# A fused attention and two-layer feed-forward kernel: second layer's first two blocks by halves, stores by batch, weights staged in other places

## The chip, the cores and the metric

One core of a Trainium2 chip. The time is that of one execution on the device, in microseconds: 1831.82 in the median of 3 runs (1831.54 to 1834.25).

## The reference

```python
# q, k, v: (8 batches, 8 heads, 576, 64), float32; chunks of 64 positions attend within themselves
scores = scale * q_c @ k_c^T;  attn = softmax(scores);  x = attn @ v_c      # x: (4608, 512)
# layer 1 (rational): w_in (512, 2048), w_out (2048, 512), both float64
h = x @ w_in
g = (a0 + a1*h + a2*h^2 + a3*h^3) / (1 + |b0|*|h| + |b1|*h^2 + 1e-6)
x = g @ w_out
# layer 2 (squared relu), same sizes, own weights
g = s * max(x @ w_in2, 0)^2 + b
out = g @ w_out2                                                            # (4608, 512) float32
```

## The kernel before

The 4608 tokens are 9 blocks of 512 (one chunk of 64 positions of all 8 batches). A step is one slice of 128 of the 2048 hidden features for one block: `mm1` makes h (12 matrix products of 128x128 by 128x512, since each float32 operand is a high and a low part and three of the four products are kept), the elementwise functions `ew_a` to `ew_e` make g and split it into gh and gl, and `mm2` adds g times w_out to four PSUM banks (12 products more). `mm2` runs `LAG` = 2 steps behind `mm1`. There are 16 slices for each block, 9 blocks and 2 layers: 288 steps, 0 to 143 for layer 1 and 144 to 287 for layer 2. All is written out by hand in program order: the loop at line 617 issues the work of each step, and each engine and each DMA queue takes its own in that order.

In layer 1, blocks 0 and 1 take turns by halves (line 380): slices 0 to 7 of block 0, then of block 1, then 8 to 15 of each. A half's sum is copied from PSUM (`evac`), stored in scratch memory `x2d`, read back (`part_load`) and added to the second half's. All other blocks, those of layer 2 too, run their 16 slices in a row. Attention of later blocks is laid between the steps of layer 1 (`att_pe`, `att_out`); its q and k come by 16 loads of 32 KB (`att_load`, line 174, SP queue) that wait for the transposes of the tile before (lines 234, 235).

Weights are float64 and are turned into float32 on the chip. Each of 32 tiles a layer goes through these: `w_stage` loads 512 KB into one of four places of tag "big", which the copies out of PSUM use too; `w_ends` (ACT, two operations) and `w_words` (DVE lines 344, 346, 347, then POOL line 348) make the float32 word in one of three places of tag "w"; `w_split` makes high and low part (ACT line 353, then DVE or POOL line 354) in the place of a layer-1 weight that is no longer read. `due` sorts the tiles by the step that needs them, `WORDS` says how many begin in each step of the first 32. A tile that begins in step i has its words made at the end of step i and is split at the end of step i + 1, behind the words of the tiles that begin there. Loads are issued on ACT's queue in the loop, ahead of ACT's `ew_a`. In steps 132 to 157 the tiles of layer 2 are converted; its blocks' inputs come back from `x2d` (`x2_load`, `x2_split`).

At a block's end `evac` is issued in the step after the block's last `mm2`. Layer 2's sums go to the output with one store of 256 KB for a bank, whose rows are 2 batches of 64 (line 444). After the loop the last block's four banks are copied and stored.

Of the kernel before, what the change touches and what calls it, by code (L numbers as in the profile page):

```python
# [51 lines left out]


WORDS = (1, 1, 1, 1, 1, 1, 1, 1, 1, 1, 1, 1, 1, 1, 1, 1, 1, 1, 1, 1, 2, 2, 1, 0, 1, 0, 3, 0, 1, 0, 0, 0)
SPLIT = "VVVVGGVVVVVVVVVVVVVVGVVGVVGVGGGG"


@with_exitstack
def tile_chunk_attention__then__rational_ffn__then__relu2_ffn(
# [70 lines left out]
    def f(t):  # L130
        return t.bitcast(F32)
# [31 lines left out]
    def att_load(n):  # L163


        h0, s0 = heads(n)
        st = att.setdefault(n, {})
        for key, src in (("q", qkv[0]), ("k", qkv[1])):
            t = st[key] = ap_.tile([P, TB], F32, tag=key, name="qk")
            t = t.rearrange("t (p g d) -> t p g d", g=2, d=32)  # L170
# [58 lines left out]
    def att_turn(n):  # L229

        st = att[n]
        qT = st["qT"] = ap_.tile([P, 2, NP, CH], F32, tag="qT", name="qT")
        kT = st["kT"] = ap_.tile([P, 2, NP, CH], F32, tag="kT", name="kT")
        V.transpose(qT.rearrange("d c p t -> d (c p t)"), st["q"])
        V.transpose(kT.rearrange("d c p t -> d (c p t)"), st["k"])
# [137 lines left out]
    def x2_split(j, kk):  # L373
        xh, xl = xt[NB + j]
        A.activation(xh[:, kk], f(xl[:, kk]), AF.Copy)
        V.tensor_tensor(out=xl[:, kk], in0=f(xl[:, kk]), in1=f(xh[:, kk]), op=ALU.subtract)
# [35 lines left out]
    part = {}  # L412

    def part_load(jj):

        part[jj] = []
        for z in range(2):
            o = ap_.tile([P, 2, TB], F32, tag="big", name="o", bufs=4)
            SP.dma_start(out=o[:, 0, :], in_=x2d[jj][2 * z])
            SP.dma_start(out=o[:, 1, :], in_=x2d[jj][2 * z + 1])  # L420
            part[jj].append(o)

    def evac(jj):
        for z in range(2):
            acc = acc_t[jj][z]
            if jj in part:
                o = part[jj][z]
                V.tensor_tensor(out=o, in0=acc, in1=o, op=ALU.add)
            else:
                o = ap_.tile([P, 2, TB], F32, tag="big", name="o", bufs=4)  # L430
                if z == 0:
                    A.activation(o, acc, AF.Copy)
                elif jj < NB:
                    V.tensor_copy(o, acc)
                else:
                    V.tensor_copy(o[:, 0], acc[:, 0])
                    A.activation(o[:, 1], acc[:, 1], AF.Copy)
            for y in range(2):
                t = 2 * z + y
                if jj < NB:  # L440
                    SP.dma_start(out=x2d[jj][t], in_=o[:, y, :])
                else:
                    s0 = (jj - NB) * CH
                    SP.dma_start(
                        out=out.rearrange("(b s) d -> b s d", b=B)[2 * t:2 * t + 2, s0:s0 + CH, :],
                        in_=o[:, y, :],
                    )
        del acc_t[jj]
# [60 lines left out]
    with tc.manual_schedule():  # L509
# [19 lines left out]
        def w_stages(phase, n, dma):  # L529
            for _ in range(n):  # L530
                if wq:
                    kind, i = wq.pop(0)
                    staged.append((phase, kind, i, w_stage(phase, kind, i, dma)))

        def w_begin(n):
            now = [staged.pop(0) for _ in range(min(n, len(staged)))]
            return [(phase, kind, i, st, w_ends(st)) for phase, kind, i, st in now]

        def w_mid(now):
            for phase, kind, i, st, w in now:  # L540
                w_words(st, w)
# [72 lines left out]
        now = words  # L614
        att_load(NV)

        for i in range(NSTEP + LAG):
# [12 lines left out]
            e = i - (N1 - MF)  # L630
            if e == KD - 1:
# [11 lines left out]
            if i >= LAG:  # L643
# [9 lines left out]
            j, kk = divmod(e, MF)
            if 0 <= j < NB and kk == 1:
                x2_load(j)
            if 0 <= j < NB and 6 <= kk < 6 + KD:
                x2_split(j, kk - 6)
# [30 lines left out]
```

## Time and profile before

| | |
|---|---|
| median of 3 runs | 1831.82 us |
| profiled execution | 1833.56 us, span 1831.8 us |
| PE busy | 1715.9 us (94%) |
| DVE | 1129.8 us (62%) |
| ACT | 857.7 us (47%) |
| POOL | 648.2 us (35%) |
| granted TensorE clock, mean | 0.972 |

The span runs from the first to the last instruction. Busy PE is not PE at its peak, as matrix products overlap. By slices of the span PE is full from about 300 to 900 us and from 1100 to 1800 us, and DVE is fullest between 950 and 1100 us. An idle engine costs nothing where another sets the time.

### The profile page before, as it was taken

How to read it: one execution, taken by the hardware profiler on the slowest of the kernel's cores; microseconds unless marked ns; L12 is line 12 of the kernel's file. 1: busy time of each engine (PE TensorE's matmuls, PEld its weight loads, DVE VectorE, ACT ScalarE, POOL GpSimd, SP SyncE). 2: the span in 40 equal slices, each digit the busy share in tenths (PEclk: the TensorE clock that was granted, in tenths of full speed). 3: DMA queues.
4: the chain of work that ended last, by engine and by line, in shares of the span. 5: the costliest groups of instructions: out<-in, count | busy, mean ns of one | idle time of the engine just before them, and what ended most of it. 6: DMA issues, size and time to landing. Idle time of an engine off the chain costs nothing.

```text
span 1831.8 us, 25181 instructions
## 1 busy us (share of the span) xinstructions
PE 1715.9 (94%) x9482; PEld 1392.6 (76%) x9482; DVE 1129.8 (62%) x1789; ACT 857.7 (47%) x1389; POOL 648.2 (35%) x561
## 2 busy tenths in 40 slices
PE   6698689999999999999998889999999999999994
PEld 4577467888888888888876668888888888888883
DVE  5899778777787778777699993333333333333331
ACT  4677456556565656565677552222223222222221
POOL 2577556555655555555677440000000000000000
PEclk8899899999999999999999999999999999999997
DMA  8522332222121222221123321010000000000000
GB/s 199 125 81 92 89 85 63 54 35 57 29 56 31 57 35 59 35 56 21 58 80 115 127 81 47 5 42 23 24 23 24 24 24 27 20 32 15 14 10 23
DMA packets 204034, 96.03 MB, mean 52 GB/s; under 512 B 179848, under 2 KB 179848, under 8 KB 203912
## 3 DMA queue, kind: packets, MB, share of 16 engines
q1 hardware_dynamic: 196136, 66.11, 14.9%
q10 hardware_dynamic: 7776, 28.32, 4.8%
q8 instruction: 74, 1.21, 0.3%
q14 instruction: 48, 0.39, 0.1%
HBM read 73.40 MB, written 20.97 MB: 52 GB/s over the span
## 4 chain that ended last, share of the span: by engine, by line
PE 75%; DVE 13%; POOL 2%; ACT 2%; issue 2%; SPq 1%; DMA 1%; ACTq 0%; DVEq 0%; POOLq 0%
PE acc L410 36%; PE h L392 12%; PE h L394 12%; PE h L393 12%; DVE w L346 2%; PE pat L303 2%; DVE w L344 2%; DVE t L473 1%; DVE w L354 1%; DVE t L489 1%; DVE t L472 1%; DVE h L488 1%; DVE w L347 1%; DVE ah L487 1%; PE pat L246 1%
## 5 line engine op out<-in xcount | busy, mean ns | idle before, releaser
L392 PE MATMUL h<-xh,w 128*128 128x512 f32 x1152 | 460.4, 400 | 0.0
L394 PE MATMUL h<-xh,w 128*128 128x512 f32 x1152 | 451.1, 392 | 2.4 <-POOL w L354 2.4
L393 PE MATMUL h<-xl,w 128*128 128x512 f32 x1152 | 451.1, 392 | 0.0
L464 ACT ACTIVATE r<-h 128x512 f32<-128x512 f32 x144 | 85.9, 596 | 509.5 <-PE h L394 503.2
L410 PE MATMUL acc<-gh,w 128*128 128x512 f32 x1152 | 293.6, 397 | 30.7 <-POOL w L354 9.8
L410 PE MATMUL acc<-w,gh 128*128 128x512 f32 x1152 | 288.8, 393 | 12.2 <-DVE gh L504 5.9
L410 PEld LDWEIGHTS acc<-gh,w 128*128 128x128 f32 x1152 | 216.0, 190 | 83.4 <-ACT gh L501 13.0
L492 DVE TENSOR_SCALAR r<-r,s_sb,b_sb 128x512 f32<-128x512 f32 x144 | 86.6, 602 | 287.6 <-ACT r L465 287.6
L410 PEld LDWEIGHTS acc<-w,gh 128*128 128x128 f32 x1152 | 217.6, 189 | 59.7 <-issue 5.8
L394 PEld LDWEIGHTS h<-xh,w 128*128 128x128 f32 x1152 | 217.6, 189 | 49.5 <-POOL w L354 2.8
L392 PEld LDWEIGHTS h<-xh,w 128*128 128x128 f32 x1152 | 218.5, 190 | 47.1
L393 PEld LDWEIGHTS h<-xl,w 128*128 128x128 f32 x1152 | 218.2, 189 | 43.5
L459 POOL TENSOR_SCALAR r<-ah,ab_sb 128x512 f32<-128x512 f32 x144 | 112.0, 777 | 298.1 <-ACT ah L457 297.9
L460 POOL TENSOR_TENSOR r<-r,ah 128x512 f32<-128x512 f32 x144 | 186.7, 1297 | 12.0
L502 POOL TENSOR_TENSOR gl<-t,gh 128x512 fp32r<-128x512 f32 x144 | 188.1, 1306 | 6.1 <-ACT gh L501 6.1
L410 PE MATMUL acc<-gl,w 128*128 128x512 f32 x576 | 158.4, 398 | 6.1 <-POOL gl L502 6.1
L479 ACT ACTIVATE ah<-r,lnb 128x512 f32<-128x512 f32 x144 | 104.0, 722 | 117.0 <-POOL r L460 116.0
L410 PE MATMUL acc<-w,gl 128*128 128x512 f32 x576 | 156.3, 394 | 0.0
L487 DVE SCALAR_TENSOR_TENSOR ah<-r,h 128x512 f32<-128x512 f32 x144 | 98.4, 683 | 86.0 <-ACT h L480 86.0
L457 ACT ACTIVATE ah<-h 128x512 f32<-128x512 f32 x144 | 85.7, 595 | 134.8 <-PE h L394 124.3
L348 POOL TENSOR_TENSOR w<-w,wst 128x512 int32<-128x512 int32 x64 | 97.7, 1527 | 111.8 <-DVE w L347 73.4
L410 PEld LDWEIGHTS acc<-gl,w 128*128 128x128 f32 x576 | 110.1, 192 | 32.0 <-POOL gl L502 8.6
(81 smaller groups left out, 2051.8 us busy)
## 6 DMA issues: line engine op xcount, KB each, us to landing
wst<-in_moe_w_out_dram ACTq DMA_DIRECT2D x30, 512.0 KB
wst<-in_moe_w_in_dram ACTq DMA_DIRECT2D x24, 512.0 KB
x2d<-o SPq DMA_DIRECT2D x44, 256.0 KB
xl<-x2d SPq DMA_DIRECT2D x36, 256.0 KB
out_dram<-o SPq DMA_DIRECT2D x36, 256.0 KB
qk<-in_q_dram SPq DMA_DIRECT2D x224, 32.0 KB
qk<-in_k_dram SPq DMA_DIRECT2D x224, 32.0 KB
vs<-in_v_dram SPq DMA_DIRECT2D x56, 128.0 KB
```

Of the source, the lines that this page charges most:

```text
L348: G.tensor_tensor(out=w, in0=w, in1=low, op=ALU.add)
L392: T.matmul(h, wh, xh[:, kk], start=kk == 0, stop=False)
L393: T.matmul(h, wh, xl[:, kk], start=False, stop=False)
L394: T.matmul(h, wl, xh[:, kk], start=False, stop=kk == KD - 1)
L410: T.matmul(o, l, r, start=first and n == 0, stop=last and n == 2)
L459: G.tensor_scalar(out=r, in0=ah, scalar1=ab_sb[:, 1:2], scalar2=ab_sb[:, 0:1], op0=ALU.mult, op1=ALU.add)
L460: G.tensor_tensor(out=r, in0=r, in1=ah, op=ALU.mult)
L464: A.activation(r, h, AF.Relu)
L479: A.activation(ah, r, AF.Ln, scale=RS, bias=lnb)
L487: V.scalar_tensor_tensor(out=t, in0=r, scalar=ONE, in1=y, op0=ALU.add, op1=ALU.mult)
L492: V.tensor_scalar(out=r, in0=r, scalar1=s_sb, scalar2=b2_sb, op0=ALU.mult, op1=ALU.add)
L502: G.tensor_tensor(out=gl, in0=g, in1=f(gh), op=ALU.subtract)
```

## The change

- Layer 2's blocks 0 and 1 take turns by halves as layer 1's do; their half sums go through `x2d` again. `WORDS2` gives the number of tiles that begin in each step from 128 on, and `X2` the steps at which the inputs of layer 2 are loaded. For its second block the inputs' low part is made on POOL.
- `evac` only copies PSUM to SBUF, at the end of the step that holds the block's last `mm2`; `store`, in the next step, adds the first half's sum where there is one (two banks on POOL, two on DVE) and issues the stores. From layer 1's last block on, the copies lie in attention's places "v", "e" and "eT".
- Output stores: two of 128 KB for a bank, one for each batch.
- `mm2_last`: the last two steps' second products run bank by bank; each bank is copied (half on ACT, half on DVE) and stored (one batch on SP's queue, one on ACT's) while the next runs.
- Weight loads are issued on SP's queue at the end of the step, layer 2's also into the places "qk" and "qkT" of attention (each now one tile for q and k). "w" has four places. `w_end` (the split) is issued before `w_mid` (the words), and its engine in layer 2 is POOL up to step 144 and DVE after that, instead of by turns.
- Layer 2's scale and bias move from DVE to ACT.

```diff
+WORDS2 = (0, 0, 0, 1, 0, 0, 0, 0, 1, 0, 1, 0, 1, 0, 1, 1, 2, 1, 2, 1, 1, 2, 1, 2, 1, 1, 1, 1, 2, 1, 1, 1, 2, 1, 1, 1)
+X2 = (1, 16, 41) + tuple(range(52, 140, 16))
...
-        st = ap_.tile([P, TB, 2], I32, tag="big", name="wst", bufs=4)
+        tag = ("big" if phase == 0 else ("big", "qk", "big", "qkT", "big", "big")[next(turn) % 6])
+        st = ap_.tile([P, TB, 2], I32, tag=tag, name="wst", bufs=4 if tag == "big" else 1)
...
-        w = ap_.tile([P, TB], I32, tag="w", name="w", bufs=3)
+        w = ap_.tile([P, TB], I32, tag="w", name="w", bufs=4)
...
-    steps = [(j, y * HF + m, m == 0, m == HF - 1) for y in range(2) for j in range(2) for m in range(HF)]
-    steps += [(j, m, m == 0, m == MF - 1) for j in range(2, 2 * NB) for m in range(MF)]
+    steps = []
+    for j0 in (0, NB):
+        steps += [(j0 + j, y * HF + m, m == 0, m == HF - 1) for y in range(2) for j in range(2) for m in range(HF)]
+        steps += [(j0 + j, m, m == 0, m == MF - 1) for j in range(2, NB) for m in range(MF)]
...
+    def out_store(jj, t, o, dma=SP):
+        s0 = (jj - NB) * CH
+        for c in range(2):
+            row = (2 * t + c) * (NT // B) + s0
+            (SP, dma)[c].dma_start(out=out[row:row + CH, :], in_=o[c * CH:(c + 1) * CH, :])
+    def mm2_last():
+        jj = steps[-1][0]
+        for z in (0, 2, 1, 3):
+            acc = acc_t[jj][z // 2][:, z % 2, :]
+            for i in (NSTEP - 2, NSTEP - 1):
+                gh, gl = g_t[i]
+                wh, wl = w_out[1, steps[i][1]]
+                t = slice(z * P, (z + 1) * P)
+                for n, (w, g) in enumerate(((wh, gh), (wl, gh), (wh, gl))):
+                    T.matmul(acc, g[:, t], w, start=False, stop=i == NSTEP - 1 and n == 2)
+            o = ap_.tile([P, 2, TB], F32, tag="big", name="o", bufs=4)[:, 0]
+            hf = slice(0, TB // 2), slice(TB // 2, TB)
+            A.activation(o[:, hf[0]], acc[:, hf[0]], AF.Copy)
+            V.tensor_copy(o[:, hf[1]], acc[:, hf[1]])
+            out_store(jj, z, o, A)
...
+    def store():
+        for jj, t, o in sums:
             if jj in part:
-                o = part[jj][z]
-                V.tensor_tensor(out=o, in0=acc, in1=o, op=ALU.add)
+                (G, V)[t // 2].tensor_tensor(out=o, in0=o, in1=part[jj][t // 2][:, t % 2], op=ALU.add)
...
+            A.activation(r, r, AF.Identity, scale=s_sb, bias=b2_sb)
...
-            V.tensor_scalar(out=r, in0=r, scalar1=s_sb, scalar2=b2_sb, op0=ALU.mult, op1=ALU.add)
...
-            if i > LAG and steps[i - 1 - LAG][3]:
-                evac(steps[i - 1 - LAG][0])
...
-            last, now = now, w_begin(WORDS[i] if i < 2 * MF else 1 if e < MF - 1 else 1 + (e % 2 == 0))
-            w_stages(i >= 2 * MF, 1 if e < MF - 1 else 1 + (e % 2 == 0), A)
+                w_stages(1, 3, SP)
+            last, now = now, w_begin(WORDS[i] if i < 2 * MF else words2)
...
+            store()
...
+            if LAG <= i < NSTEP and steps[i - LAG][3]:
+                evac(steps[i - LAG][0])
             for x in range(4):
                 att_out(2 * i, x)
+            w_end(last, (V if e > MF else G) if i >= 2 * MF else V if SPLIT[i] == "V" else G)
             w_mid(now)
-            w_end(last, None if i >= 2 * MF else V if SPLIT[i] == "V" else G)
+            w_stages(i >= 2 * MF, 1 if i < 2 * MF else words2, SP)
...
-        evac(steps[-1][0])
+        mm2_last()
```

## Rows read from the trace of the kernel before

**Rows 1.** Busy time by stretch: us, then each engine's, clock, DMA share, GB/s.

```profile
47.90:318.11 270.21, 222.74 (x1369) 174.44 (x1368) 231.79 (x354) 169.22 (x281) 170.82 (x143) 0.92 0.33 87
913.70:992.44 78.74, 69.96 (x289) 54.38 (x288) 75.06 (x98) 57.41 (x95) 61.10 (x49) 0.98 0.26 83
992.44:1093.72 101.28, 84.96 (x337) 66.59 (x336) 93.74 (x123) 56.59 (x99) 50.50 (x35) 0.93 0.35 118
1093.72:1806.53 712.81, 712.80 (x3145) 589.90 (x3143) 245.02 (x434) 189.66 (x309) 4.51 (x3) 1.00 0.07 23
1806.53:1831.80 25.27, 0.00 (x0) 0.00 (x0) 0.69 (x1) 1.20 (x2) 0.00 (x0) 0.55 0.11 42
```

**Rows 2.** Chain of waits, its end: start, duration, what.

```profile
1792.93 2.72 PE acc L410 x12
1798.37 8.17 PE acc L410 x36
```

**Rows 3.** Groups by line, 1010 to 1093.7: busy us, mean ns, idle before.

```profile
L492 DVE TENSOR_SCALAR r<-r,s_sb,b_sb 128x512 f32<-128x512 f32 x12 | 13.8, 1153 | 0.7 <-ACT r L465 0.7
L348 POOL TENSOR_TENSOR w<-w,wst 128x512 int32<-128x512 int32 x18 | 25.8, 1433 | 46.3 <-DVE w L347 22.8 <-ACT w L353 9.8 <-issue 5.1
L346 DVE TENSOR_SCALAR w<-w 128x512 int32<-128x512 int32 x17 | 13.3, 782 | 0.6
L347 DVE SCALAR_TENSOR_TENSOR w<-wst,w 128x512 int32<-128x512 int32 x18 | 12.5, 692 | 0.6
L353 ACT ACTIVATE w<-w 128x512 fp32r<-128x512 f32 x16 | 9.4, 615 | 0.0
L505 DVE TENSOR_TENSOR gl<-r,gh 128x512 fp32r<-128x512 f32 x12 | 9.2, 765 | 1.2
L354 DVE TENSOR_TENSOR w<-w,w 128x512 fp32r<-128x512 f32 x9 | 9.0, 1001 | 1.3 <-ACT w L353 1.3
L504 DVE CAST gh<-r 128x512 fp32r<-128x512 f32 x12 | 8.7, 725 | 1.2
L344 DVE TENSOR_SCALAR w<-w 128x512 f32<-128x512 f32 x17 | 7.1, 420 | 0.2 <-ACT w L337 0.2
```

**Rows 4.** Groups by line, 913.7 to 992.4.

```profile
L344 DVE TENSOR_SCALAR w<-w 128x512 f32<-128x512 f32 x11 | 10.9, 995 | 0.0
L346 DVE TENSOR_SCALAR w<-w 128x512 int32<-128x512 int32 x11 | 10.5, 957 | 0.4
L347 DVE SCALAR_TENSOR_TENSOR w<-wst,w 128x512 int32<-128x512 int32 x11 | 9.5, 865 | 0.4
L354 DVE TENSOR_TENSOR w<-w,w 128x512 fp32r<-128x512 f32 x5 | 3.4, 682 | 0.0
```

**Rows 5.** Timeline after PE's end, DVE and SP's queue: start, duration, what, idle before.

```profile
1806.56 0.69 DVE L436 COPY o<-acc 128x512 f32<-128x512 f32 x1 [4.75 <-PE acc L410]
1807.16 10.08 SPq L444 DMA_DIRECT2D out_dram<-o  x4
```

**Rows 6.** Busy time by stretch, during output stores and during scratch loads.

```profile
1808.31:1830.46 22.15, 0.00 (x0) 0.00 (x0) 0.00 (x0) 0.00 (x0) 0.00 (x0) 0.51 0.13 47
1538.10:1542.50 4.40, 4.40 (x21) 3.65 (x20) 1.67 (x3) 0.45 (x1) 0.00 (x0) 1.00 0.73 238
```

**Rows 7.** Timeline of SP's queue, ACT and DVE around steps 18 and 21.

```profile
193.93 4.96 SPq L174 DMA_DIRECT2D qk<-in_k_dram  x8
...
202.44 0.60 ACT L457 ACTIVATE ah<-h 128x512 f32<-128x512 f32 x1 [9.84 <-DMA x2d<-o]
...
203.74 0.69 DVE L472 TENSOR_TENSOR t<-t,h 128x512 f32<-128x512 f32 x1 [6.53 <-ACT t L458]
...
230.61 0.67 ACT L337 ACTIVATE w<-wst 128x512 f32<-128x512 f32 x1 [7.04 <-POOL w L354]
...
233.02 0.69 DVE L472 TENSOR_TENSOR t<-t,h 128x512 f32<-128x512 f32 x1 [2.92 <-ACT t L458]
```

**Rows 8.** Waits of DVE, 255 to 320: total us, times, longest.

```profile
DVE o L428 <- DMA o<-x2d: 4.3, 2, 2.4
```

More of the change, by code (lines that the diff above doesn't have):

```diff
@@ L166, in att_load @@
         h0, s0 = heads(n)
[L167 to L170, printed above, removed]
+        qk = ap_.tile([P, 2, TB], F32, tag="qk", name="qk")
+        att.setdefault(n, {})["qk"] = qk
+        for x, src in enumerate(qkv[:2]):
+            t = qk[:, x].rearrange("t (p g d) -> t p g d", g=2, d=32)
             for y in range(4):
@@ L231, in att_turn @@
         st = att[n]
[L232 to L235, printed above, removed]
+        qkT = ap_.tile([P, 2, TB], F32, tag="qkT", name="qkT")
+        for x in range(2):
+            V.transpose(qkT[:, x], st["qk"][:, x])
+            st["qk"[x] + "T"] = qkT[:, x].rearrange("d (c p t) -> d c p t", c=2, p=NP)
     def att_S(n, t=None):
@@ L375, in x2_split @@
         A.activation(xh[:, kk], f(xl[:, kk]), AF.Copy)
-        V.tensor_tensor(out=xl[:, kk], in0=f(xl[:, kk]), in1=f(xh[:, kk]), op=ALU.subtract)
-    steps = [(j, y * HF + m, m == 0, m == HF - 1) for y in range(2) for j in range(2) for m in range(HF)]
-    steps += [(j, m, m == 0, m == MF - 1) for j in range(2, 2 * NB) for m in range(MF)]
+        (G if j == 1 else V).tensor_tensor(out=xl[:, kk], in0=f(xl[:, kk]), in1=f(xh[:, kk]), op=ALU.subtract)
+    steps = []
+    for j0 in (0, NB):
+        steps += [(j0 + j, y * HF + m, m == 0, m == HF - 1) for y in range(2) for j in range(2) for m in range(HF)]
+        steps += [(j0 + j, m, m == 0, m == MF - 1) for j in range(2, NB) for m in range(MF)]
     def mm1(i):
@@ L410, in mm2 @@
                 T.matmul(o, l, r, start=first and n == 0, stop=last and n == 2)
-    part = {}
+    part, halves = {}, set()
     def part_load(jj):
@@ L418, in part_load @@
             o = ap_.tile([P, 2, TB], F32, tag="big", name="o", bufs=4)
-            SP.dma_start(out=o[:, 0, :], in_=x2d[jj][2 * z])
-            SP.dma_start(out=o[:, 1, :], in_=x2d[jj][2 * z + 1])
+            SP.dma_start(out=o[:, 0, :], in_=x2d[jj % NB][2 * z])
+            SP.dma_start(out=o[:, 1, :], in_=x2d[jj % NB][2 * z + 1])
             part[jj].append(o)
-    def evac(jj):
-        for z in range(2):
-            acc = acc_t[jj][z]
+    def out_store(jj, t, o, dma=SP):
[3 more added lines that the diff above has]
+            (SP, dma)[c].dma_start(out=out[row:row + CH, :], in_=o[c * CH:(c + 1) * CH, :])
@@ new lines, in tile_chunk_attention__then__rational_ffn__then__relu2_ffn @@
+    sums = []
+    def evac(jj):
+        for t in range(4):
+            acc = acc_t[jj][t // 2]
+            if jj >= NB - 1:
+                o = ap_.tile([P, TB], F32, tag=("v", "v", "e", "eT")[t], name="o", bufs=(2, 2, 1, 1)[t])
+                i = acc[:, t % 2]
+            elif t % 2 == 0:
+                o, i = ap_.tile([P, 2, TB], F32, tag="big", name="o", bufs=4), acc
+            else:
+                sums.append((jj, t, o[:, 1]))
+                continue
+            if t < 2:
+                A.activation(o, i, AF.Copy)
+            else:
+                V.tensor_copy(o, i)
+            sums.append((jj, t, o if jj >= NB - 1 else o[:, 0]))
+        del acc_t[jj]
@@ L426, in evac @@
+    def store():
+        for jj, t, o in sums:
             if jj in part:
-                o = part[jj][z]
-                V.tensor_tensor(out=o, in0=acc, in1=o, op=ALU.add)
-            else:
[L430 to L448, printed above, removed]
+                (G, V)[t // 2].tensor_tensor(out=o, in0=o, in1=part[jj][t // 2][:, t % 2], op=ALU.add)
@@ L450, in ew_a @@
+            if jj < NB or jj < NB + 2 and jj not in halves:
+                SP.dma_start(out=x2d[jj % NB][t], in_=o)
+            else:
+                out_store(jj, t, o)
+        halves.update(jj for jj, _, _ in sums)
+        sums.clear()
     def ew_a(i):
@@ L615, in tile_chunk_attention__then__rational_ffn__then__relu2_ffn @@
         att_load(NV)
-        for i in range(NSTEP + LAG):
+        for i in range(NSTEP + 1):
             if i < NSTEP:
                 mm1(i)
-            if i > LAG and steps[i - 1 - LAG][3]:
-                evac(steps[i - 1 - LAG][0])
             att_out(2 * i - 1, 0)
@@ L630, in tile_chunk_attention__then__rational_ffn__then__relu2_ffn @@
             e = i - (N1 - MF)
-            if e == KD - 1:
+            words2 = WORDS2[e] if 0 <= e < len(WORDS2) else 0
+            if e == 0:
                 wq.extend(due(1))
-            last, now = now, w_begin(WORDS[i] if i < 2 * MF else 1 if e < MF - 1 else 1 + (e % 2 == 0))
-            w_stages(i >= 2 * MF, 1 if e < MF - 1 else 1 + (e % 2 == 0), A)
+                w_stages(1, 3, SP)
+            last, now = now, w_begin(WORDS[i] if i < 2 * MF else words2)
             if i < NSTEP:
@@ L641, in tile_chunk_attention__then__rational_ffn__then__relu2_ffn @@
                 ew_b(i)
+            store()
             att_pe(2 * i)
-            if i >= LAG:
+            if LAG <= i < NSTEP:
                 mm2(i - LAG)
             att_pe(2 * i + 1)
+            if LAG <= i < NSTEP and steps[i - LAG][3]:
+                evac(steps[i - LAG][0])
             for x in range(4):
                 att_out(2 * i, x)
+            w_end(last, (V if e > MF else G) if i >= 2 * MF else V if SPLIT[i] == "V" else G)
             w_mid(now)
-            w_end(last, None if i >= 2 * MF else V if SPLIT[i] == "V" else G)
-            if i - LAG + 2 in (3 * HF - 1, 4 * HF - 1):
+            w_stages(i >= 2 * MF, 1 if i < 2 * MF else words2, SP)
+            if (i - LAG + 2) % N1 in (3 * HF - 1, 4 * HF - 1):
                 part_load(steps[i - LAG + 2][0])
[L653 to L657, printed above, removed]
-        evac(steps[-1][0])
+            for j, at in enumerate(X2):
+                if e == at:
+                    x2_load(j)
+                if 2 <= e - at < 2 + KD:
+                    x2_split(j, e - at - 2)
+        mm2_last()
 _INS = ['q', 'k', 'v', 'moe_w_in', 'moe_w_out', 'moe_a', 'moe_b', 'moe2_w_in', 'moe2_w_out', 'moe2_s', 'moe2_b']
```

2 lines of the change are left out of this document (removed).

## The prediction

> **What bounds the kernel now.** I read the split into stretches first. By the page's slices PE is busy at full clock from some 320 to 910 us, and so it is from 1093.72 to 1806.53; what is not so lies in four places [rows 1]: the opening to step 33 (47.90 to 318.11), the end of layer 1 (steps 132 to 143, up to 992.44), the first fourteen steps of layer 2 (144 to 157, up to 1093.72), and 25.27 us at the end in which PE does nothing. In the two middle ones DVE is busy 75.06 of 78.74 and 93.74 of 101.28 us, which is a bound engine, and the clock dips to 0.93.
>
> Then the chain of waits, for the price of a step. From 1093.72 on it is PE alone, a group of twelve second products every 5.44 us, and the last 36 follow without a gap for 8.17 us [rows 2]. So 5.44 us is the floor of a step without attention, and the excess can be read off: 78.74 - 12 x 5.44 = 13.5 us and 101.28 - 14 x 5.44 = 25.1 us, together 38.6 us. The cause is the conversion of layer 2's 32 weight tiles on top of the elementwise work.
>
> Last the end. PE stops at 1806.53, the last copy out of PSUM is short, the four output stores are issued from 1807.16 on [rows 5], and from 1808.31 to 1830.46 the DMA engines are busy to a share of 0.13, that is 2.1 of 16, at 47 GB/s. Four loads of the same 256 KB from scratch memory ran at 0.73 and 238 GB/s, 1 MB in 4.40 us [rows 6].
>
> **Transition: conversion at half the rate.** Blocks 0 and 1 of layer 2 now need 32 tiles within their 32 steps instead of block 0 within 16, and the list gives 6 tiles to steps 131 to 143 and 26 to steps 144 to 163.
>
> Layer 1's part. DVE was busy 75.06 us for 12 steps with 12 tiles [rows 1]. One tile's integer work was 0.995 + 0.957 + 0.865 = 2.82 us there [rows 4]. Taking 6 tiles away, and their split, which POOL now does for tiles begun before step 144, leaves 75.1 - 16.9 - about 4 = 54 us, and a thirteenth step adds less than 5: 59 of 13 x 5.44 = 70.7 us. DVE is no longer the bound; I take 0 to 1 us of stall for 13.5.
>
> Layer 2's part. A tile's integer work is 0.420 + 0.782 + 0.692 = 1.89 us here, its split 0.68 (as in layer 1) to 1.00, the step's own work 0.725 + 0.765 = 1.49 once the scale and bias are ACT's [rows 3]. So 26 x 1.89 + 26 x 0.84 + 20 x 1.49 = 49.1 + 21.8 + 29.8 = 100.7 us, plus some 6 for the last layer-1 step and the PSUM copies (two of 0.69 each at three block ends [rows 5]): 107 of 20 x 5.44 = 108.8 us. That is all but full. One cost is new: the split now stands in front of the next tile's integer work, so DVE waits for POOL's add (1.43) and ACT's copy (0.615) [rows 3] with only its own 1.49 to fill them: 0.56 us in each of 14 steps that follow a single tile, 8 us if DVE runs back to back. Against it, second products run two steps behind, which absorbs several us, and the scaling that leaves DVE had cost it 1.153 in each step [rows 3]. Bounds: 0, and the old 25.1 unchanged. I take 4 us, near the ledger. Gain of the transition: 38.6 - 4 = 34.6 us.
>
> Its other parts cost nothing while PE binds. The scaling on ACT, taken like ACT's copy of a tile of this size, 0.615 [rows 3], comes 144 times where ACT is busy 190 of 713 us [rows 1]; g is late by nothing that the two steps of distance don't hold, and without them it would be by some 0.1 us a step, ACT's price less DVE's undisturbed one. The eight extra part sums, their 16 stores and 16 loads fall into steps where DVE is 34% busy and the DMA engines 7% [rows 1]. POOL takes half of the sums; it is idle there. Three tiles are staged ahead, in two more places, so a tile's load has two steps to land.
>
> **End.** The last two steps' 24 products run bank by bank, so three banks leave while PE still works. After PE's end: half a bank on each of ACT and DVE, some 0.43 (a whole one takes 0.69 [rows 5]), issue 0.5, first packet 1.15 us after issue (1807.16 to 1808.31 [rows 5, 6]), the last 256 KB some 0.9 (a quarter of 4.40 [rows 6] is 1.1), and the 1.34 us from the last packet to the span's end: 4.3 instead of 25.27, gain 21.0. Bounds: 22 if the landing is quicker; 4 if the stores stay at 47 GB/s, since the first one would then start some 4 us earlier and 1 MB still needs 22.15 us. The store by batch has 64 rows, which no row shows; the scratch transfers, whose outermost dimension is also the partitions, are the nearest, so I take 21.
>
> The row shows 2.1 engines for an output store and about 12 for a scratch load [rows 6]. The Trainium skill, DMA: Bandwidth & Descriptors, Rules for kernel authors, says two transfers to disjoint partition halves aren't worth it, as both use the same 16 engines; by that the two half stores would be as slow as one and the gain would be 4. The same section says an outermost dimension below 16 confines a DMA to that many engines; by that the old store, 2 batches outermost, was held to 2, and 64 rows free it: gain 21. The trace's 2.1 speaks for the second.
>
> **Opening.** Here the change moves work from queue to queue. ACT issued the weight loads; at 192.6 to 202.4 it stood 9.84 us behind one whose place a scratch store still held, and DVE then 6.53 us behind ACT. At 230.61 ACT had waited 7.04 us for the third conversion buffer, DVE 2.92 [rows 7]. Both waits go: loads move to SP, and there is a fourth buffer. DVE was the bound there (231.79 of 270.21 us [rows 1]), so up to 9.5 us are free, and 4.3 more where DVE waited for a part sum's load [rows 8], since PSUM is now copied out first and the sum made later, half of it on POOL. But on SP the load stands behind the 16 small loads of the next attention tile, which start when DVE's transposes end and of which the second eight alone took 4.96 us [rows 7], some 9 us in all; I add 4.4 us to land, an estimate from [rows 6]. At step 17 the tile is needed two steps later, when DVE has some 10 us of other work: a new wait of 3 to 4 us for 6.53. At step 20 the next tile is needed one step later: 13 us against some 4 of work, a new wait of 8 to 9 for 2.92. So the two nearly cancel; with the part sums and the earlier copy at block ends I take a gain of 4 us, between +6 (lost) and -14 (all waits gone).
>
> Blocks 2 to 8 of layer 1 are PE's; the PSUM copy there is issued earlier, with a first half of a step as cover as before: 0.
>
> **Sum.** The profiled execution took 1833.56 us (span 1831.80). 1833.56 - 34.6 - 21.0 - 4 = 1774.0; it stood 1.74 above the median of the runs, so against 1831.82 I forecast 1772 us.
>
> **Rivals.**
> - The split's wait bites: DVE is back to back through the transition and each of the 26 tiles costs the wait in full, so that some 16 us of the 38.6 come back: 1772 + 14 = 1786. For: the ledger is 107 of 108.8. Against: the slack of two steps, and single tiles alternate with pairs, which hide it.
> - The opening gains all its idle time, and the split in front fills the time in which a tile's first operation on DVE is slowed beside POOL: -14 instead of -4, 1762. For: that operation took 0.995 in layer 1 and 0.420 in layer 2, where POOL has less to do [rows 3, 4]. Against: SP's 16 loads.
> - The stores don't spread: 1772 + 17 = 1789. For: no row shows a store of 64 rows. Against: a transfer as contiguous as it ran on 12 engines [rows 6].
> - Slower than before: the same wait of POOL's add, ACT's copy and ACT's queue in front of DVE's split hits both conversions, the opening too, where DVE is the bound. At most 1.43 + 0.62 = 2.05 us for each of 24 + 32 = 56 tiles, 115 us, 1772 + 115 = 1887; it decides against the change above 1.07 us per tile (60 / 56). Against: in the old order ACT made that copy while DVE was still at the step's own work, which stays ahead of the split.
>
> **Chances.** Forecast, 1760 to 1781: 0.67. Split's wait 0.14, opening 0.10, stores 0.05, slower 0.03, and 0.01 for losses that just cancel the gain. The 8-in-10 range takes in the first rival and the second, to 1789 above and 1758 below. A measurement of this kernel can tell some 0.2% (3.7 us) from no change: faster 0.96, same 0.01, slower 0.03.
>
> **What would show it.** Steps of 5.44 us from 144 on, with under 6 us of excess up to 163; DVE over 90% busy there; the output stores at a DMA share well above 0.13, and under 5 us between PE's end and the span's; at steps 19 and 21 an ACT that waits for a weight load behind SP's attention loads. Wrong: an excess over 15 us in the transition, stores still at 47 GB/s, or an opening that is longer than 280 us.

## The result, and the profile after

1785.55 us in the median of 4 runs (1783.53 to 1787.64) against 1831.68 for the kernel before: ratio 0.9748, 95% interval 0.9728 to 0.9768. The forecast was 1772, in a range of 1758 to 1789. In the text TensorE is PE of the rows, VectorE is DVE, ScalarE ACT, GpSimd POOL. The profiled execution took 1787.20 us (span 1785.4). Lines of the changed kernel: `mm1` 399 to 401, `mm2` 417, conversion 342 to 353, split 358 and 359, `ew_e` 539 and 540, the last copies 450 and 451.

First the stretches, in the columns of [rows 1]: opening to step 33, steps 132 to 143, steps 144 to 157, the rest to TensorE's end, what is behind it, and 5 us of the last stores.

```profile
47.13:320.57 273.44, 228.09 (x1370) 173.78 (x1368) 234.51 (x355) 170.35 (x282) 172.26 (x145) 0.93 0.33 87
916.16:981.44 65.28, 65.28 (x290) 54.05 (x289) 56.50 (x77) 47.57 (x76) 51.27 (x44) 1.00 0.12 40
981.44:1067.32 85.88, 79.41 (x337) 63.62 (x336) 81.88 (x109) 67.05 (x112) 38.91 (x30) 0.98 0.45 148
1067.32:1780.20 712.88, 712.88 (x3145) 589.84 (x3143) 207.17 (x350) 304.64 (x463) 17.03 (x13) 1.00 0.11 31
1780.20:1785.40 5.20, 0.01 (x1) 0.00 (x0) 0.54 (x2) 0.38 (x1) 0.00 (x0) 0.83 0.46 130
...
1778.50:1783.50 5.00, 1.71 (x8) 1.07 (x6) 0.85 (x2) 0.77 (x2) 0.00 (x0) 1.00 0.65 169
```

| part | before | after | change | forecast |
|---|---|---|---|---|
| start of step 34 (opening) | 318.11 | 320.57 | +2.46 | -4 |
| steps 132 to 143, excess over 5.44 each | 13.46 | 0.00 | -13.46 | -12.5 to -13.5 |
| steps 144 to 157, excess | 25.12 | 9.72 | -15.40 | -21 |
| behind TensorE's end | 25.27 | 5.20 | -20.07 | -21.0 |
| sum | | | -46.5 | -59.6 |

The excess is what a stretch takes beyond 5.44 us a step. All else is step for step the same. The 13.1 us that are missing are 6.5 of the opening, 5.7 of layer 2's start and 0.9 of the end.

**Layer 2's start.** The groups by line from 995 to 1067.3, as in [rows 3]:

```profile
L540 DVE TENSOR_TENSOR gl<-r,gh 128x512 fp32r<-128x512 f32 x12 | 19.8, 1650 | 1.1
L359 DVE TENSOR_TENSOR w<-w,w 128x512 fp32r<-128x512 f32 x16 | 14.6, 929 | 1.4 <-ACT w L358 0.6
L352 DVE SCALAR_TENSOR_TENSOR w<-wst,w 128x512 int32<-128x512 int32 x17 | 11.8, 692 | 0.6
L351 DVE TENSOR_SCALAR w<-w 128x512 int32<-128x512 int32 x16 | 10.9, 683 | 0.5
L349 DVE TENSOR_SCALAR w<-w 128x512 f32<-128x512 f32 x16 | 6.7, 418 | 0.0
L539 DVE CAST gh<-r 128x512 fp32r<-128x512 f32 x13 | 5.5, 420 | 0.0
```

DVE's own work in a step is 0.420 + 1.650 = 2.07 us, where the forecast had 1.49. Pieces of a timeline (start, duration, what) show why: POOL's add runs from 1014.55 to 1015.86; the subtraction, begun at 1014.76, ends 0.55 us after it. Undisturbed it takes 0.69.

```profile
1010.43 2.36 DVE L359 TENSOR_TENSOR w<-w,w 128x512 fp32r<-128x512 f32 x2
...
1014.24 0.42 DVE L539 CAST gh<-r 128x512 fp32r<-128x512 f32 x1
1014.76 1.65 DVE L540 TENSOR_TENSOR gl<-r,gh 128x512 fp32r<-128x512 f32 x1
...
1009.91 1.73 POOL L381 TENSOR_TENSOR xl<-xl,xh 128x512 fp32r<-128x512 f32 x1
...
1014.55 1.31 POOL L353 TENSOR_TENSOR w<-w,wst 128x512 int32<-128x512 int32 x1 [2.91 <-DVE w L352]
```

The cast was already running when the add began, and it took its 0.42 us. So it is from 995 to 1067.3 throughout: all 20 operations of DVE that took over 1.4 us were begun while one of POOL's was running, and the 17 during which one of POOL's began all took 0.42. Four of the 20 are splits (1.56 to 1.77 us, the twelve others under 0.8; the first of the two at 1010.43 is one). They stand beside POOL's L381, the low part of the second block's input, which the change itself gave to POOL.

Who waited there (total us, times, longest): TensorE for DVE, and DVE's split for ACT's copy hardly at all, 0.6 us.

```profile
PE acc L417 <- DVE o L471: 3.2, 2, 2.1
PE h L401 <- DVE w L359: 1.5, 1, 1.5
PE acc L417 <- DVE w L359: 1.3, 1, 1.3
...
DVE w L359 <- ACT w L358: 0.6, 2, 0.5
```

Of the 9.72 us 4.35 lie in step 146, where TensorE waits 2.1 us for DVE's copy out of PSUM, which stands behind a subtraction of 1.59 us.

**Opening.** Weight loads behind SP's 16 attention loads (the later of two such places), and what stood behind them (timeline of SP's queue, ACT and DVE, as [rows 7]):

```profile
219.90 3.78 SPq L177 DMA_DIRECT2D qk<-in_q_dram  x8
223.73 3.90 SPq L177 DMA_DIRECT2D qk<-in_k_dram  x8
227.67 0.92 SPq L330 DMA_DIRECT2D wst<-in_moe_w_out_dram  x2
...
204.41 0.68 ACT L342 ACTIVATE w<-wst 128x512 f32<-128x512 f32 x1 [5.61 <-DMA wst<-in_moe_w_out_dram]
...
231.50 0.66 ACT L342 ACTIVATE w<-wst 128x512 f32<-128x512 f32 x1 [11.30 <-DMA wst<-in_moe_w_out_dram]
...
206.83 0.69 DVE L510 TENSOR_TENSOR t<-t,h 128x512 f32<-128x512 f32 x1 [4.20 <-ACT t L495]
...
233.89 0.69 DVE L510 TENSOR_TENSOR t<-t,h 128x512 f32<-128x512 f32 x1 [6.18 <-ACT t L495]
```

**End.** The last copies and stores (timeline). TensorE ends at 1780.21; ACT issues the third bank's store first, until 1780.84, and begins its last copy 0.68 us after that end. The two halves of a bank are copied one after the other: the trace has DVE's half released by ACT's (0.99), perhaps because both write one tile; that was not tried.

```profile
1780.34 0.50 ACTq L435 DMA_DIRECT2D out_dram<-o  x1
1780.89 0.38 ACT L450 ACTIVATE o<-acc 128x256 f32<-128x256 f32 x1 [1.45 <-DVE o L451]
1781.76 0.50 ACTq L435 DMA_DIRECT2D out_dram<-o  x1
...
1781.30 0.42 DVE L451 COPY o<-acc 128x256 f32<-128x256 f32 x1 [0.99 <-ACT o L450]
```

### The profile page after: what moved, and what is told of

It is laid out like the page before. It is cut to its first block, busy times and chain, and to the rows that moved or that the text cites. A ratio compares the mean times of both kernels' runs of the same rounds, so it can differ in the third digit from the quotient of the medians.

```text
span 1785.4 us, 25329 instructions
## 1 busy us (share of the span) xinstructions
PE 1711.3 (96%) x9482; PEld 1388.7 (78%) x9482; DVE 1066.3 (60%) x1673; ACT 975.6 (55%) x1542; POOL 644.2 (36%) x563
## 4 chain that ended last, share of the span: by engine, by line
PE 78%; DVE 10%; SPq 3%; ACT 3%; POOL 2%; issue 2%; DMA 1%; ACTq 0%; DVEq 0%; POOLq 0%
PE acc L417 37%; PE h L399 13%; PE h L401 12%; PE h L400 12%; PE pat L306 2%; SPq L153 1%; DVE w L351 1%; DVE w L349 1%; DVE w L359 1%; DVE w L352 1%; SPq L177 1%; DVE t L527 1%; DVE t L510 1%; DVE t L511 1%; DVE h L526 1%
## 5 line engine op out<-in xcount | busy, mean ns | idle before, releaser
L417 PE MATMUL acc<-w,gh 128*128 128x512 f32 x1136 | 282.8, 391 | 4.7 <-DVE o L471 3.2
L539 DVE CAST gh<-r 128x512 fp32r<-128x512 f32 x144 | 61.5, 427 | 336.1 <-ACT r L503 336.0
L417 PEld LDWEIGHTS acc<-w,gh 128*128 128x128 f32 x1136 | 213.6, 188 | 50.7 <-DVE o L471 4.0
L537 POOL TENSOR_TENSOR gl<-t,gh 128x512 fp32r<-128x512 f32 x144 | 193.7, 1345 | 2.0 <-ACT gh L536 1.9
L417 PE MATMUL acc<-w,gl 128*128 128x512 f32 x568 | 152.1, 390 | 0.0
L353 POOL TENSOR_TENSOR w<-w,wst 128x512 int32<-128x512 int32 x64 | 85.0, 1327 | 131.4 <-DVE w L352 90.4
L540 DVE TENSOR_TENSOR gl<-r,gh 128x512 fp32r<-128x512 f32 x144 | 120.8, 839 | 18.5 <-PE acc L417 2.7
```

What stands on the lines that cost most here:

```text
L537: G.tensor_tensor(out=gl, in0=g, in1=f(gh), op=ALU.subtract)
L540: V.tensor_tensor(out=gl, in0=g, in1=f(gh), op=ALU.subtract)
```

## Experiments

Theory: in the opening the order on SP's queue took back what the removed waits gave; in layer 2's start POOL's add hinders DVE as before, only at another operation; the stores' form and the halves made the gain. Each kernel was timed beside the kernel before on its chip, whose median there was 1831.50 to 1832.55 us.

**The stores.** The kernel before with the new form of store alone:

```diff
-    SP.dma_start(out=out.rearrange("(b s) d -> b s d", b=B)[2 * t:2 * t + 2, s0:s0 + CH, :], in_=o[:, y, :])
+    for c in range(2):
+        row = (2 * t + c) * (NT // B) + s0
+        SP.dma_start(out=out[row:row + CH, :], in_=o[c * CH:(c + 1) * CH, y, :])
```

> The kernel before with one part of the change alone: each bank's output store is two of 64 rows by 512, one for each batch, both on SP's queue; nothing else is changed, so that the last 24 products still run in two steps and the four banks are copied after them. Theory (the old store form was what held the transfer to 2.1 of 16 DMA engines): the stretch behind TensorE's end falls from 25.27 to 6 to 9 us at a DMA share above 0.5, and the time is 1812 to 1816. Rival (64 rows are no wider than 2 batches, and the end was won by running the last steps bank by bank): the stores still move at about 47 GB/s, and the time is 1829 to 1834.

1814.87 us, ratio 0.9898 (0.9884 to 0.9913). TensorE ends at 1805.16, the span 8.54 us later, against 25.27. The stretches behind TensorE's end and of the stores:

```profile
1805.16:1813.70 8.54, 0.00 (x0) 0.00 (x0) 0.69 (x1) 1.21 (x2) 0.00 (x0) 0.74 0.54 123
1807.00:1812.50 5.50, 0.00 (x0) 0.00 (x0) 0.00 (x0) 0.00 (x0) 0.00 (x0) 0.71 0.82 188
```

And the changed kernel with the old form, which is the same edit backwards, in `out_store`:

> The changed kernel, but each bank's output goes out as one store with 2 batches as its outermost dimension, on SP's queue, as before; the last two steps still run bank by bank. Theory (the store's form is worth nearly all of the end): 1 MB still needs 22 us from the first bank's copy, some 8 us before TensorE's end, so that the stretch behind its end is 15 to 20 us instead of 5.20, and the time is 1796 to 1801. Rival (bank by bank hides the stores): the stretch is under 9 us, the time under 1790.

1804.26 us, 0.9831 (0.9814 to 0.9849): 3 us above the expected range, of which 2.2 are a later step 34 (322.73 for 320.57), which this edit can't make. The first store is issued 3.2 us before TensorE's end (1779.26), not the 8 that I had expected. TensorE ends at 1782.42, the span 20.88 us later, at 2.1 engines (0.13 x 16) and 49 GB/s as before:

```profile
1782.42:1803.30 20.88, 0.00 (x0) 0.00 (x0) 0.42 (x1) 0.38 (x1) 0.00 (x0) 0.57 0.12 47
1781.00:1802.00 21.00, 1.42 (x7) 0.84 (x5) 0.85 (x2) 0.77 (x2) 0.00 (x0) 0.60 0.13 49
```

So running bank by bank brings 4.4 us without the new form (25.27 to 20.88, the prediction's lower bound of 4) and 3.3 with it (8.54 to 5.20); the form brings 16 to 17. The rule of the Trainium skill, DMA: Bandwidth & Descriptors, Rules for kernel authors, that a small outermost dimension confines a DMA, agrees with 2 batches on 2.1 engines and 64 rows on 13.

**The attention's loads on SP.**

```diff
-                        att_load(n + 1)
+                        late.append(n + 1)
...
             w_stages(i >= 2 * MF, 1 if i < 2 * MF else words2, SP)
+            while late:
+                att_load(late.pop(0))
```

> The changed kernel, but in the loop the 16 small loads of the next attention tile are issued behind the step's weight load and scratch loads instead of ahead of them. Theory (queue order on SP): ACT's wait of 11.30 us at 231.50 for a weight load goes, and the 4.20 and 6.18 us in which DVE waited for ACT at 206.83 and 233.89 with it; step 22 falls from 15.08 to under 9 us, step 34 starts some 8 us earlier (about 312 instead of 320.57), and the time is about 1777 (1773 to 1780). Rival (the load is late for its place or for the transfer itself, or the opening is DVE's work and the wait only stands where DVE would be late anyway): step 34 starts within 2 us of 320.57 and the time is 1784 to 1788. Second rival: the attention tile's q and k are now late, DVE's transposes or TensorE's scores wait for them, and the time is over 1790.

In this edit the loads stand behind the weight load, but still ahead of the part sums' loads. 1776.57 us, 0.9687 (0.9672 to 0.9701). Step 22 took 8.81 us instead of 15.08 and step 34 began at 309.91. DVE's busy time in the opening is what it was, 234.82 against 234.51 us; the 10.85 us by which the stretch is shorter were idle time of DVE. ACT's wait for weight loads from 180 us on fell from 16.9 to 2.0. The opening (columns of [rows 1]) and that wait:

```profile
47.32:309.91 262.59, 222.70 (x1369) 171.69 (x1368) 234.82 (x355) 170.68 (x282) 172.47 (x145) 0.94 0.34 89
...
ACT w L342 <- DMA wst<-in_moe_w_out_dram: 2.0, 4, 0.9
```

**No halves in layer 2.**

```diff
-    for j0 in (0, NB):
-        steps += [... by halves for blocks j0 and j0 + 1, the others in a row]
+    steps = [... by halves for blocks 0 and 1]; all others in a row, layer 2's too
-WORDS2 = (0, 0, 0, 1, 0, 0, 0, 0, 1, 0, 1, ...)
+WORDS2 = (0,) * 4 + (1,) * 12 + (2, 1) * 7
...
```

With the halves go the part sums of layer 2 (their loads and their stores to `x2d`), and the steps of `X2` are again 16 apart.

> The changed kernel, but layer 2's first two blocks run their 16 slices in a row, so its 32 weight tiles begin in steps 132 to 157 by the old rule (one a step, then one and two by turns). All else stays: the scale and bias on ACT, the split ahead of the words, loads on SP, four word places. Theory (turns by halves make the transition's gain): layer 1's last twelve steps have some 72 us of DVE work again for 65.3 and lose 7 to 10 us, layer 2's first fourteen have 18 tiles of some 2.8 us and 2.07 us of their own work a step, 80 to 86 us, and lose 8 to 14 instead of 9.7; with the pairs in a row the time is 1793 to 1806. Rival (the scale and bias on ACT and the order of split and words made it, and halves are a detail): the time is within 4 us of the changed kernel's 1785.55.

1803.01 us, 0.9831 (0.9817 to 0.9846), 17.5 above the changed kernel. Steps 132 to 143 took 79.57 us, 14.3 over 12 x 5.44, where 7 to 10 were expected; steps 144 to 157 lost 13.0 (89.14 - 76.16), steps 158 to 163 another 0.9. Step 34 began at 317.61, 3.0 earlier than in the changed kernel, though the opening's code is the same. The first row is steps 132 to 143, the second steps 144 to 159:

```profile
913.19:992.76 79.57, 70.64 (x289) 54.27 (x288) 75.88 (x93) 57.32 (x96) 68.01 (x55) 0.98 0.26 85
992.76:1093.71 100.95, 92.96 (x385) 73.67 (x384) 94.12 (x125) 74.56 (x123) 44.17 (x33) 0.97 0.33 105
```

**POOL's add.** Left out of layer 2's conversions:

```diff
-    def w_words(st, w):
+    def w_words(st, w, add):
...
-        G.tensor_tensor(out=w, in0=w, in1=low, op=ALU.add)
+        if add:
+            G.tensor_tensor(out=w, in0=w, in1=low, op=ALU.add)
...
-                w_words(st, w)
+                w_words(st, w, phase == 0)
```

> The changed kernel, but the last operation of layer 2's 32 word conversions, POOL's integer add of the low bits, is left out, so that the weights of layer 2 lack their lowest bits; all else stays. Theory (the add beside it is what makes VectorE's subtraction 1.65 instead of 0.69 us, and DVE's split 0.93): both fall to 0.70 or less in the first fourteen steps of layer 2, their excess over 5.44 us a step falls from 9.72 to under 3 us, and the time is 1776 to 1780. Rival (the subtraction is slow for ACT's write into its operand or for anything else than POOL): it stays above 1.3 us and the excess above 7, as the latency of the add alone is covered; 1782 to 1786.

1777.87 us, 0.9705 (0.9691 to 0.972). The excess of steps 144 to 157 fell from 9.72 to 1.50 us and the subtraction (now L541) to 0.693; the split fell to 0.757 only, not to 0.70, as POOL's low part of the input is still there. Steps 144 to 157, then the groups by line from 995 us on:

```profile
982.00:1059.66 77.66, 76.84 (x337) 62.84 (x336) 65.24 (x108) 66.12 (x111) 12.15 (x9) 1.00 0.50 166
...
L360 DVE TENSOR_TENSOR w<-w,w 128x512 fp32r<-128x512 f32 x16 | 11.8, 757 | 7.8 <-ACT w L359 7.8
...
L541 DVE TENSOR_TENSOR gl<-r,gh 128x512 fp32r<-128x512 f32 x11 | 7.6, 693 | 1.0
```

**The scaling** back on DVE:

```diff
-            A.activation(r, r, AF.Identity, scale=s_sb, bias=b2_sb)
...
+        else:
+            V.tensor_scalar(out=r, in0=r, scalar1=s_sb, scalar2=b2_sb, op0=ALU.mult, op1=ALU.add)
```

> The changed kernel, but layer 2's scale and bias are made on VectorE again (one two-scalar operation in each step, ahead of gh), and ACT's Identity pass is gone. Theory (POOL's integer add slows whichever VectorE operation runs beside it, so the 1.65 us of the split's subtraction and the 1.15 us that the scaling had before are the same loss in two places): the scaling takes 1.0 to 1.2 us in the first fourteen steps of layer 2, the subtraction falls from 1.65 to 0.75 to 0.9, the step's own work is about 2.6 us instead of 2.07, and 14 to 20 steps lose 8 to 11 us: 1793 to 1797. Rival (the durations belong to the operations, as my ledger had it): the subtraction stays at 1.65, own work is 2.8 to 3.2, and the time is 1801 to 1808. Second rival (VectorE isn't what holds these steps): 1784 to 1787.

1792.78 us, 0.9785 (0.9769 to 0.9801), 0.2 below the theory's range; but the place of the loss was another than I had written. Not the scaling is slow here (0.541) but the cast behind it (groups by line from 995 us on, then a piece of the timeline). The subtraction's 1.022 is a mean of seven quick ones and four of 1.6 us, which were begun beside POOL's L381.

```profile
L541 DVE CAST gh<-r 128x512 fp32r<-128x512 f32 x12 | 16.2, 1350 | 1.1
L542 DVE TENSOR_TENSOR gl<-r,gh 128x512 fp32r<-128x512 f32 x11 | 11.2, 1022 | 1.0
...
L529 DVE TENSOR_SCALAR r<-r,s_sb,b_sb 128x512 f32<-128x512 f32 x12 | 6.5, 541 | 0.0
...
1018.24 1.35 DVE L541 CAST gh<-r 128x512 fp32r<-128x512 f32 x1
...
1017.91 1.39 POOL L353 TENSOR_TENSOR w<-w,wst 128x512 int32<-128x512 int32 x1 [3.51 <-DVE w L352]
```

So three kernels have the loss in three operations (before: the scaling, 1.153 [rows 3]; here the cast; after: the subtraction), and without the add most of it is gone: it belongs to whichever DVE begins while POOL is at its operation. The Trainium skill, SBUF — State Buffer, Who interferes with whom, has VectorE and POOL share a pair of ports that one of them holds for a whole instruction; the subtraction that ends 0.55 us after the add agrees.

**An even list of tiles.** Eight tiles in layer 1's last steps, then one a step:

```diff
-WORDS2 = (0, 0, 0, 1, 0, 0, 0, 0, 1, 0, 1, 0, 1, 0, 1, 1, 2, 1, 2, 1, 1, 2, 1, 2, 1, 1, 1, 1, 2, ...)
+WORDS2 = (0, 0, 0, 1, 0, 1, 0, 1, 0, 1, 0, 1, 0) + (1,) * 27
```

> The changed kernel with another list alone: eight of layer 2's 32 weight tiles begin in layer 1's last steps instead of six, one each in steps 131, 133, 135, 137, 139, 141, 142 and 143, and then exactly one in each of steps 144 to 167, instead of one and two by turns up to 163. Theory (what is left of the stall in layer 2's start is VectorE's work, and its worst steps are those with two tiles: two of 1.79 + 0.93 and 2.07 of its own are 7.5 us against 5.44, one tile is 4.8): the excess of steps 144 to 157 falls from 9.72 to 1 to 3 us, and the time is 1777 to 1780. Rival (the chain of VectorE's words, POOL's add, ACT's copy and VectorE's split is what waits, and with one tile in every step nothing fills it): excess 7 to 14, 1783 to 1790.

1782.02 us, 0.9729 (0.9714 to 0.9743), 2 us above the expected range. Steps 144 to 157 lose 3.09 us instead of 9.72, but steps 132 to 143 lose 1.89 that they had not lost. By the spans (1785.4 and 1780.4) it is 5.0 us. The subtraction stays at 1.652, and DVE's split now waits 4.2 us for ACT's copy, which TensorE doesn't feel: steps 147 to 157 take 5.44 us each (steps 144 to 157, then groups by line):

```profile
983.41:1062.66 79.25, 77.39 (x338) 62.75 (x336) 70.81 (x93) 60.63 (x100) 35.06 (x26) 1.00 0.38 128
...
L540 DVE TENSOR_TENSOR gl<-r,gh 128x512 fp32r<-128x512 f32 x13 | 21.5, 1652 | 1.2
L359 DVE TENSOR_TENSOR w<-w,w 128x512 fp32r<-128x512 f32 x13 | 12.5, 958 | 5.0 <-ACT w L358 4.2
```

**Words ahead of the split,** as in the kernel before (`w_mid(now)` in front of `w_end`):

> The changed kernel with the words of the tiles begun in a step made ahead of the split of the tile before, as in the kernel before, instead of behind it; everywhere, the opening too. Theory (VectorE's split hardly waits: 0.6 us in all for ACT's copy in layer 2's start, so the turn is nearly free): 1783 to 1789, the waits of the split for ACT's copy zero, those of TensorE for the split a little longer, as a tile is ready 1.8 us later. Rival of my prediction (the split in front costs its wait for POOL's add and ACT's copy at every tile, in both conversions): without it the time falls to 1770 to 1781. Rival on the other side (tiles are due just in time, and the split in front is part of the gain): 1790 to 1800.

1782.57 us, 0.973 (0.9717 to 0.9743): between the theory, which it misses by 0.4, and the first rival. Step 34 begins 3.5 us earlier. In layer 2's start step 148 alone takes 11.63 us, as TensorE waits for a tile that is split later, while most of the other stalls there are gone; the excess is 8.52. So the turn moves loss about and costs some 3 us, not the 115 of the prediction's slower rival. Waits of TensorE for DVE's split from 965 to 1070:

```profile
PE h L401 <- DVE w L359: 4.0, 1, 4.0
```

**Together.** Deferred loads and the even list:

> The changed kernel with the attention tile's loads behind the step's weight load (as in the first run) and the even list of weight tiles together. The two concern stretches 600 us apart, so by the theory of both they add: step 34 at about 310 us, excess of layer 2's first fourteen steps 1 to 3 us, 1767 to 1772. By the rival on the list (the chain waits): 1774 to 1781.

1772.61 us, 0.9676 (0.966 to 0.9692), 0.6 over the theory's range: 12.9 us below the changed kernel, where the two alone had 9.0 and 3.5. Then the same with the eight tiles of layer 1 in every second step (called e10 below):

```diff
-WORDS2 = (0, 0, 0, 1, 0, 1, 0, 1, 0, 1, 0, 1, 0) + (1,) * 27
+WORDS2 = (0, 0, 1, 0, 1, 0, 1, 0, 1, 0, 1, 0, 1, 0, 1, 1) + (1,) * 24
```

> As the kernel with the deferred loads and the even list, but the eight tiles of layer 1's last steps stand in every second step (130, 132, 134, 136, 138, 140, 142) and 143 instead of odd steps up to 139 and then 141, 142, 143. Theory (three tiles in a row on top of layer 1's own work overload VectorE, and that is where the even list lost 1.9 us in steps 137 to 143 and 2.7 in 144 and 145): these steps fall to 5.44 to 5.8 us, the transition's excess from 8 to 2 to 4 us, time 1767 to 1770. Rival (eight tiles beside layer 1's own work are too many wherever they stand): 1771 to 1774.

1770.75 us, 0.9664 (0.9651 to 0.9677), between theory and rival. Steps 136 to 143 still take 5.50 to 5.81 us each; the transition loses 1.73 + 2.09 us where it had lost 1.82 + 3.06 (not the 8 that I had written). Of the 1.9 us, 1.4 are an earlier step 34, which the list can't make, so that spreading is worth some 1 us at most. And this with one split moved (`SPLIT[20]` from G to V):

> The kernel of the run before it, with one split of the opening (that issued in step 20) on VectorE instead of POOL. In the run with deferred loads TensorE stood 3.17 us in step 21 behind POOL's split, which POOL began 2.9 us after ACT's copy since it was at attention's normalisation. Theory (that queue ends the wait): step 21 falls from 13.9 to 10.5 to 12 us and the time by 2 to 3 us. Rival (VectorE is as full as POOL there; its own work then ends last): within 1 us of the run before it.

1770.23 us, 0.9662 (0.9649 to 0.9675): no change. Step 21 fell to 11.11 as the theory said (16.04 in e10), but steps 22 and 23 took 11.66 and 8.98 instead of 8.82 and 6.75. Last, e10 with the words first in steps 0 to 31 alone:

```diff
+            if i < 2 * MF:
+                w_mid(now)
             w_end(last, ...)
-            w_mid(now)
+            if i >= 2 * MF:
+                w_mid(now)
```

> The kernel with deferred loads and spread tiles (e10), and in the first 32 steps alone the words ahead of the split, as in the kernel before; the transition keeps the split ahead. In the run with words first everywhere step 34 started 3.5 us earlier than in the changed kernel. Theory (VectorE's split waits in the opening for POOL's add and ACT's copy, apart from the queue on SP, so the two gains add): step 34 at 305 to 307.5 us instead of 309.77, time 1766 to 1768.5. Rival (the words first won there only what the deferred loads win too): within 1 us of e10's 1770.75.

1767.35 us (1766.82 to 1767.71), 0.9649 (0.9636 to 0.9662), step 34 at 306.69: faster than both kernels, 18.2 us below the changed one. The gain adds, but not by the mechanism I named. In e10 DVE's split waited 0.6 us for ACT's copy in the whole opening. Of the 3.1 us by which step 34 is earlier, 1.1 are an earlier step 0; steps 0 to 7 take 1.9 more, steps 8 to 17, where DVE works nearly back to back, 3.4 less (61.27 us for 64.68), the rest 0.5 less. Step 8 alone makes 2.4 of the 3.4. It took 7.82 us in e10, at a granted clock of 0.78, which is a mean of the clock's two levels (1.2 and 2.4 GHz), after a step in which TensorE was busy for 6.91 of 8.70 us. Here it took 5.44 at 1.00, and steps 6 and 7 have 0.89 and 0.91 instead, TensorE being busy for 7.36 of 9.45 us in step 6. Steps 8 to 17 in e10 and here:

```profile
120.16:184.84 64.68, 60.40 (x241) 45.33 (x242) 62.19 (x88) 48.04 (x79) 46.68 (x38) 0.97 0.26 87
120.93:182.20 61.27, 56.69 (x241) 44.48 (x240) 59.63 (x85) 46.45 (x76) 45.16 (x37) 1.00 0.26 86
```

Steps 12 to 17, at the full clock in both, take 1.0 us less (39.27 for 40.28). The split takes 0.685 instead of 0.759 in steps 8 to 17, which is 0.7 us over ten of them; what makes the rest stays open. The longest wait left is TensorE's for one split on POOL in step 21:

```profile
PE acc L417 <- POOL w L359: 7.8, 1, 7.8
```

## Why the prediction was right, and where it was off

The time lies in the stated range, but above the 1760 to 1781 that was given 0.67. It is in the range because that took in the first rival, which is luck, since that rival's wait did not make the loss. Two of the signs failed: the excess up to step 163 is 9.72 us, not under 6, and TensorE's end is 5.20 us before the span's, not under 5.

- **Layer 1's end: right.** 13.46 us of stall are gone; DVE is busy 56.50 of 65.28 us there (forecast 59 of 70.7 for thirteen steps). The run without halves, with the same order and queues, has 14.3 us of stall there: the halves did it, with the list of tiles that they allow.
- **Layer 2's start: the mechanism right, one term mis-sized.** The term is the step's own work of DVE, "0.725 + 0.765 = 1.49 us once the scale and bias are ACT's"; it measured 2.07. I took the 1.153 of the scaling as that operation's price and its departure as a gain in full, though the same ledger held POOL's add, and 1.153 is far from the 0.4 that a like one-input operation takes (L344 [rows 3]). With the scaling gone the subtraction meets the add. 0.58 us in 14 steps is 8 us; the forecast had 4 of stall where 9.72 came, and 1.50 remain without the add. The slow subtraction costs that much only where two tiles fall into a step: with one a step it still takes 1.652 us and the excess is 3.09. Moving the scale to ACT was still worth 7.2 us (1792.78 to 1785.55); by the profiles 6.2 us lie in layer 2's steps, and 2.0 are a later step 34, which that edit can't make.
- **The split's wait: refuted as the price.** I gave it up to 8 us here and 14 as the first rival; it was 0.6 us. The time came out at that rival's 1786 for another reason. What kept the wait short is what I had against it: the step's own work and pairs of tiles lie in between. With the pairs gone, in the even list, it is 4.2 us, and TensorE still doesn't wait.
- **Opening: the waits right, the gain of 4 us wrong.** ACT waits behind SP's attention loads from 198.8 and from 220.2 us, in steps 19 and 21, as forecast; DVE lost 4.20 and 6.18 us for 6.53 and 2.92 [rows 7]. That "the two nearly cancel" holds in TensorE's steps 18 to 22 together: 57.10 us before, 56.50 after. What failed is the next clause, "with the part sums and the earlier copy at block ends I take a gain of 4 us": step 34 began 2.46 us later. The stretches of steps in five kernels, in us; "both" has the loads deferred and the words first (and another list of tiles, which works from step 130 on):

| steps | before | after | loads deferred | words first | both |
|---|---|---|---|---|---|
| start of step 0 | 47.90 | 47.13 | 47.32 | 46.82 | 47.23 |
| 0 to 17 | 137.10 | 138.34 | 138.04 | 135.13 | 134.97 |
| 18 to 22 | 57.10 | 56.50 | 47.78 | 58.61 | 50.65 |
| 23 and 24 | 14.47 | 14.95 | 14.96 | 14.43 | 13.67 |
| 25 to 28 | 31.19 | 33.33 | 31.44 | 31.76 | 29.80 |
| 29 to 33 | 30.34 | 30.32 | 30.37 | 30.35 | 30.36 |
| start of step 34 | 318.11 | 320.57 | 309.91 | 317.09 | 306.69 |

With both orders turned the opening gains 11.4 us, where I had 14 with all waits gone. The loads on SP take 10.7 of that back (320.57 - 309.91), about the 11 to 13 of new waits that I had. The split in front of the words takes another 3.1 (e10's step 34 at 309.77 against 306.69), most of it by step 17; the four kernels with the loads deferred and the split in front began step 34 at 309.77 to 311.17. That term the sum had at nothing in the opening. The slower rival named it, by a wait that is not there, and the second rival had it as a gain; by which path it costs stays open.

At the block ends no gain is left, and why is open. Around the first block end with part sums, steps 25 to 28 went from 31.19 to 33.33 us. The 4.3 us for which DVE waited for the loads [rows 8] are gone, but PSUM's copy now stands on DVE in front of attention's subtraction, and TensorE waited 2.0 us for that in step 25 (11.30 us for 7.58), while POOL makes two sums (2.54 us) ahead of its own next operation. In the changed kernel, DVE's copy and the subtraction behind it, and TensorE's wait:

```profile
265.61 1.23 DVE L471 COPY o<-acc 128x1024 f32<-128x1024 f32 x1 [1.30 <-PE acc L417]
266.75 0.68 DVE L319 TENSOR_TENSOR xl<-pat,xh 128x512 fp32r<-128x512 f32 x1
...
PE pat L249 <- DVE xl L319: 2.6, 2, 2.0
```

But the copies and sums are the same in the kernels with the loads deferred or the words first, and there the four steps lose 0.25 and 0.57 us, not 2.14. So the copy's place alone doesn't make the loss; it was not tried alone. A us or two can't be told there anyhow: in the five kernels of these experiments whose opening is the changed kernel's own, step 34 began at 317.61 to 322.73, which nearly reaches the 317.09 with the words first.

- **End: right, 0.9 us off.** The store's form was nearly the whole question, and both runs on it decide it as the prediction chose. The 0.9 us are ACT's store in front of its last copy (0.68) and the half copies that run in turn, 0.38 + 0.42 where I had one of 0.43; from the last issue on it is 3.63 us where the forecast had 3.9.

## What to carry to other kernels

An operation whose mean is well above that of its like can be a sign of what runs beside it: here taking it away, or putting it back, moved the loss to the next one, and leaving out the other engine's operation ended most of it. When an operation changes queue or place, price it by what is queued ahead of it and by what it is now queued ahead of, not by the wait that goes alone. The cost of these output stores was set by their outermost dimension; look at the DMA share of the last microseconds before making anything else shorter.

## What was not expected of the hardware

The cast with one input was held up by POOL's add as the subtraction with two was: 0.420 us where the add began behind it, 1.350 where the add was already running. A store of 2 x 64 x 512 moved at 49 GB/s and the same bytes as two of 64 x 512 at 188.
